# Causal attention with a hard-swish feed-forward on one core: VectorE's bit operations by way of PSUM, the first groups' remainders on GpSimd, batch 0's attention later in the order

## The chip, the cores and the metric

The program runs on one core of a Trainium2 chip. The metric is the device time of one execution, in microseconds. The median of three runs of the kernel before is 700.54 us (698.27 to 700.77). PE is TensorE, DVE VectorE, ACT ScalarE, POOL GpSimd, and SP the engine that issues the DMAs.

## The reference, cut to what matters

```python
def _attn_ref(q, k, v):                    # each (4, 12, 448, 64): batch, head, token, dim
    scores = (1.0 / np.sqrt(64)) * np.matmul(q, k.transpose(0, 1, 3, 2))
    scores = np.where(mask, -1000000000.0, scores)      # causal
    scores = scores - np.max(scores, axis=-1, keepdims=True)
    attn = np.exp(scores)
    attn = attn / (np.sum(attn, axis=-1, keepdims=True) + 1e-09)
    return np.matmul(attn, v)

def _moe_ref(x, w_in, w_out):              # x (1792, 768), w_in (768, 2048), w_out (2048, 768)
    h = x @ w_in
    g = h * np.clip(h + 3.0, 0.0, 6.0) / 6.0
    return g @ w_out
```

## The kernel before

The 1792 tokens go in five groups. Group 0 holds the first 112 tokens of each of the four batches (448 columns); groups 1 to 4 hold the other 336 tokens of one batch each. Heads go in 6 pairs, two of 64 dims on the 128 partitions.

**Attention.** `first_pair` (L294) does one head pair of group 0 for all four batches: scores and mask into two PSUM banks `s` (PE), row maxima on DVE, exponentials on ACT, sums, `inverse` (L365: add 1e-9 and reciprocal, once for each head), the scaling `pr` (L372, POOL or DVE), transposes (L381) through banks `mo`, copies to `pt` (L237 on ACT or L240 on DVE), products with v (L394) into the bank `av`. `pair` (L405) does one pair of a batch's other 336 tokens: six score tiles in banks `s` (L420), a masked maximum on DVE (L437), exponentials on ACT (L444), reciprocals on DVE (L453, L454), scaling on POOL (L466), transposes (L477) through banks `s`, copies to `pt`, products with v (L496) into `av`. There are 24 such pairs, 6 for each batch. `x_split` (L276) then turns `av` into two parts: `xh`, rounded to fp32r (ACT), and the remainder `xl = av - xh` (DVE, L249).

**Feed-forward.** `group` (L553) multiplies 16 chunks of `w_in` (768 columns) by x, and 24 chunks of `w_out` (512 columns) by g. Each product is done in three (`triple`, L547): wh·xh (L549), wh·xl (L550), wl·xh (L551), which makes 576 products for each group. Behind a chunk of `w_in` stand ACT (`r`, ReLU of h + 3), DVE (L579: r = min(r, 6)·h), the rounded `gh` and the remainder `gl = r - gh` (L249).

**Weights.** The inputs are stored as float64 words. In group 0, `weights` (L508) loads a chunk as pairs of int32 (`wd`, 1536 or 1024 columns) and makes float32 of it with three integer operations on DVE (`bits`, L527): L531 shifts and masks the high words into `wf`, L533 ors in the sign bits, L535 ors in the low words' bits. L533 and L535 each read `wd` and `wf`, both in SBUF. Then `wh` is rounded on ACT (L237), `wl = wf - wh` is taken on POOL (L249), and SP writes `wf` to DRAM (`kept`). Groups 1 to 4 load the kept float32 chunks and do no bit operations.

**What sets the order.** `Flow` is a planner that runs when the program is built. Every operation has a key (a due time), the engines that may do it with a cost for each (`{"D": 1, "P": (1.9, .7)}` means DVE, or POOL at 1.9 times the cost and only .7 us after it became ready), and its buffers. The planner gives each engine a fixed list, which the chip follows in order. Group g has keys from 96·g; chunk i of `w_in` has 96·g + 3·i. Pair n of the 24 has key T_REST + 16·n with T_REST = -22, its loads come 24 earlier, and its products with v 13 later. Eight PSUM banks are shared out as `s` 5, `av` 1, `mo` 2.

Of the kernel before, what the change touches and what calls it, by code (L numbers as in the profile page):

```python
# [48 lines left out]

T_FIRST, T_REST, T_LOAD, T_W, T_WLOAD = -66, -22, -24, 9, 9  # L50


BUFS = dict(
    gh=1, gl=1, prow=3, wf=2, r=2, ob=2, qr=3, kr=3, vr=3, wh=3, wl=3, pr3=4, pr2=4, pr1=4,
    pt0=4, pt1=4, pt2=4, wd=4, xh=9, xl=9,
)
BANKS = dict(s=5, av=1, mo=2)

# [131 lines left out]
def tile_causal_attention_hardswish_moe(ctx: ExitStack, tc: tile.TileContext, q, k, v, w_in, w_out, out):  # L190
# [24 lines left out]
    def f(x):  # L215
        return x.bitcast(F32)
# [59 lines left out]
    def x_split(key, g, p, av, n):  # L276
        xh, xl = buf("xh", [128, S], F32R), buf("xl", [128, S], F32R)
        x_t[g, p] = xh, xl
        move(key, n, lambda: ap(xh)[:, :n], lambda: ap(av)[:, :n], [(av, 0)], [(xh, 0)], {"A": 1, "D": (1, .5)})
        minus(  # L280
            key + .01, n, lambda: ap(xl)[:, :n], lambda: ap(av)[:, :n], lambda: f(ap(xh)[:, :n]),
            [(av, 0), (xh, 0)], [(xl, 0)], {"D": 1},
        )
# [8 lines left out]
    def first_pair(p):  # L292
# [112 lines left out]
    def pair(n):  # L405
        b, p = divmod(n, NPAIR)
        t = T_REST + 16 * n
        qr, kr, vr = buf("qr", [128, R]), buf("kr", [128, S]), buf("vr", [C, NC_, 2, D])
# [50 lines left out]
        for e in range(2):  # L459
# [11 lines left out]
            for a, js in enumerate(((0,), (1,), (2, 3))):  # L471
# [3 lines left out]
                def turn(e=e, blocks=blocks, tp=tp):  # L475
# [32 lines left out]
    def weights(g, i, t, early):  # L508
# [3 lines left out]
        if g:  # L512
            dma(t - T_W - T_WLOAD, 512 * n, lambda: f(ap(wd))[:, :n], lambda: kept[i, :, :n], [("kept", i)], [(wd, 0)])
            w, wk = lambda: f(ap(wd))[:, :n], (wd, 0)
        else:
            m, r = divmod(i - NF, 4)
            src = w_in[i] if i < NF else w_out[m, :, 4 * r:4 * r + 4]
            dma(
                early if early else t - T_W - T_WLOAD, 1024 * n,
                lambda: ap(wd)[:, :2 * n].rearrange("p (n k) -> p n k", k=256), lambda: src, [], [(wd, 0)],  # L520
            )
            wf = buf("wf", [128, 768])
            w, wk = lambda: ap(wf)[:, :n], (wf, 0)

            def bits(a):  # L527
                ti = w().bitcast(I32)
                low, high = ap(wd)[:, 0:2 * n:2], ap(wd)[:, 1:2 * n:2]
                if a == 0:  # L530
# [22 lines left out]
    def group(g):  # L553
# [3 lines left out]
        for i in range(NF):  # L557
# [3 lines left out]
            for part in range(3):  # L561
                def products(part=part, wh=wh, wl=wl, acc=acc):
# [13 lines left out]
            )  # L576
            one(
                t, {"D": 1}, elem(n),
                lambda _, r=r, acc=acc: nc.vector.scalar_tensor_tensor(  # L579
                    ap(r)[:, :n], ap(r)[:, :n], 6.0, ap(acc)[:, :n], ALU.min, ALU.mult  # L580
                ),
                [(acc, 0)], [(r, 0)],
            )
# [80 lines left out]
```

## Time and profile before

| | us |
|---|---|
| median of 3 runs | 700.54 |
| the profiled execution, its own time | 699.9 |
| its span, first to last instruction | 698.2 |
| PE busy | 664.2 (95%) |
| DVE busy | 443.3 (63%) |
| ACT busy | 356.3 (51%) |
| POOL busy | 224.7 (32%) |

The shares are means over stages that differ. The first product of group 0 starts 44.6 us after the span's start, the first product of group 0 with `w_out` at 145.9 us, and the first product of group 1 at about 238 us. After that every chunk of weights is a plain load. Matmuls overlap, so that a busy PE is not PE at its peak.

### The profile page before, as it was taken

To read this page: it belongs to the slowest core of one execution; us is meant where nothing else is said; L and a number is where in the kernel's file an instruction comes from. 1 tells how busy PE (TensorE), PEld (TensorE's weight loads), DVE (VectorE), ACT (ScalarE), POOL (GpSimd) and SP (SyncE) were. 2 spreads that over 40 slices of the span, in tenths; PEclk is the share of its full clock that TensorE was granted. 3 is DMA by queue.
4 is the path that set the end of the run, shared out by engine and by line. 5 is a ranking of instruction groups with operands and counts; after the bars stand their busy time and mean duration, and the time that the engine had idled before them with its cause. 6 is when DMAs were issued, how large, how long until landed. Compare 5 with 4: busy or idle time off the path is not lost.

```text
span 698.2 us, 11840 instructions
## 1 busy us (share of the span) xinstructions
PE 664.2 (95%) x4236; PEld 572.1 (82%) x4236; DVE 443.3 (63%) x875; ACT 356.3 (51%) x844; POOL 224.7 (32%) x267
## 2 busy tenths in 40 slices
PE   6788987989999899999999999999999999999998
PEld 4566766768767778889988889988889899999998
DVE  5898998996779466554555666454576643466532
ACT  4665554454235455665555666445576554444332
POOL 2445465553536432322213342201344310022000
PEclk9899999999999999999999999999999999999999
DMA  9958767667787544345564333545533244744452
GB/s 236 289 162 253 227 180 209 194 198 236 220 258 234 162 127 130 88 123 158 164 176 133 115 108 112 173 134 170 158 114 93 77 124 130 209 145 119 138 161 74
DMA packets 60347, 113.63 MB, mean 163 GB/s; under 512 B 14976, under 2 KB 26880, under 8 KB 60288
## 3 DMA queue, kind: packets, MB, share of 16 engines
q1 hardware_dynamic: 60288, 112.88, 54.7%
q8 instruction: 33, 0.54, 0.3%
q14 instruction: 26, 0.21, 0.1%
HBM read 94.77 MB, written 18.09 MB: 162 GB/s over the span
## 4 chain that ended last, share of the span: by engine, by line
PE 66%; POOL 0%; ACT 0%; issue 0%
PE mo L549 18%; PE mo L551 17%; PE mo L550 17%; PE s L420 5%; PE av L496 5%; PE s L477 4%; POOL pr L466 0%; POOL wl L249 0%; ACT ob L237 0%
## 5 line engine op out<-in xcount | busy, mean ns | idle before, releaser
L249 DVE TENSOR_TENSOR wl<-wd,wh 128x512 fp32r<-128x512 f32 (+1 forms) x153 | 124.9, 817 | 151.9 <-ACT wh L237 147.5
L237 ACT CAST wh<-wd 128x512 fp32r<-128x512 f32 (+1 forms) x160 | 112.8, 705 | 151.6 <-PE mo L550 88.7
L549 PE MATMUL mo<-xh,wh 128*128 128x336 f32 (+1 forms) x480 | 164.5, 343 | 3.7 <-DVE r L579 3.7
L549 PE MATMUL mo<-gh,wh 128*128 128x336 f32 (+1 forms) x480 | 164.2, 342 | 0.0
L551 PE MATMUL mo<-gh,wl 128*128 128x336 f32 (+1 forms) x480 | 158.6, 330 | 4.1 <-POOL wl L249 4.0
L550 PE MATMUL mo<-gl,wh 128*128 128x336 f32 (+1 forms) x480 | 157.2, 327 | 0.0
L551 PE MATMUL mo<-xh,wl 128*128 128x336 f32 (+1 forms) x480 | 157.0, 327 | 0.0
L550 PE MATMUL mo<-xl,wh 128*128 128x336 f32 (+1 forms) x480 | 156.6, 326 | 0.0
L466 POOL TENSOR_SCALAR pr<-pr,prow 112x224 f32<-112x224 f32 x144 | 102.4, 730 | 156.3 <-PE mo L550 89.6
L549 PEld LDWEIGHTS mo<-xh,wh 128*128 128x128 f32 x480 | 90.4, 188 | 16.8 <-issue 7.8
L549 PEld LDWEIGHTS mo<-gh,wh 128*128 128x128 f32 x480 | 91.1, 190 | 11.1 <-issue 5.8
L551 PEld LDWEIGHTS mo<-gh,wl 128*128 128x128 f32 x480 | 90.9, 189 | 8.2 <-POOL wl L249 6.6
L550 PEld LDWEIGHTS mo<-gl,wh 128*128 128x128 f32 x480 | 91.2, 190 | 1.3
L551 PEld LDWEIGHTS mo<-xh,wl 128*128 128x128 f32 x480 | 90.4, 188 | 1.8 <-POOL wl L249 0.3
L550 PEld LDWEIGHTS mo<-xl,wh 128*128 128x128 f32 x480 | 90.5, 189 | 1.2
L444 ACT ACTIVATE pr<-s,prow 112x448 f32<-112x448 f32 (+1 forms) x144 | 77.1, 540 | 26.7 <-DVE prow L437 26.7
L249 POOL TENSOR_TENSOR wl<-wf,wh 128x512 fp32r<-128x512 f32 (+1 forms) x39 | 64.5, 1654 | 73.1 <-ACT wh L237 63.1
L437 DVE CUSTOM_DVE_ANT_0 s<-s,mask 112x448 f32<-112x448 f32 (+1 forms) x144 | 69.9, 529 | 10.5 <-PE s L420 10.5
L244 POOL TENSOR_SCALAR gh<-r 128x336 fp32r<-128x336 f32 x52 | 24.5, 471 | 158.8 <-DVE r L579 141.6
L237 ACT CAST wh<-wf 128x512 fp32r<-128x512 f32 (+1 forms) x40 | 28.2, 706 | 76.3 <-DVE wf L535 63.2
L477 PE MATMUL s<-ident,pr 112*112 112x112 f32 x432 | 58.8, 264 | 7.6 <-POOL pr L466 4.8
L237 ACT COPY pt<-s 112x336 f32<-112x336 f32 x133 | 53.5, 440 | 23.1 <-PE s L477 22.0
(57 smaller groups left out, 706.0 us busy)
## 6 DMA issues: line engine op xcount, KB each, us to landing
wd<-kept_w SPq DMA_DIRECT2D x64, 384.0 KB, 3.3
wd<-kept_w SPq DMA_DIRECT2D x96, 256.0 KB, 2.7
wd<-in_w_in_dram SPq DMA_DIRECT2D x16, 768.0 KB, 5.2
wd<-in_w_out_dram SPq DMA_DIRECT2D x24, 512.0 KB, 4.6
kept_w<-wf SPq DMA_DIRECT2D x16, 384.0 KB, 5.5
kept_w<-wf SPq DMA_DIRECT2D x24, 256.0 KB, 4.7
kr<-in_k_dram SPq DMA_DIRECT2D x24, 224.0 KB, 3.4
vr<-in_v_dram SPq DMA_DIRECT2D x24, 224.0 KB, 3.1
```

Of the source, the lines that this page charges most:

```text
L237: nc.scalar.copy(o(), i()) if scale is None else nc.scalar.mul(o(), i(), scale)
L244: nc.gpsimd.tensor_scalar(o(), i(), 1.0, 1.0, ALU.mult, ALU.mult)
L249: (nc.gpsimd if e == "P" else nc.vector).tensor_tensor(o(), a(), b(), ALU.subtract)
L420: nc.tensor.matmul(ap(ps[e, i])[:C, :w], ap(qr)[m, C * (i - 1):C * i], ap(kr)[m, :w], start=True, stop=True)
L437: lambda _, e=e, i=i, w=w, dst=dst: nc.vector.tensor_tensor_reduce(dst(), dst(), mask[:, S - w:], -0.125, 3.0e38, ALU.add, ALU.min, ap(st) ...
L444: lambda _, e=e, i=i, dst=dst: nc.scalar.activation(ap(pr[e, i]), dst(), ACTF.Exp, bias=ap(st)[:, e, i:i + 1], scale=-1.0, accum_out=ap(st ...
L466: nc.gpsimd.tensor_scalar(x, x, r, 1.0, ALU.mult, ALU.mult)
L477: nc.tensor.transpose(ap(tp)[:C, C * o:C * o + C], ap(pr[e, i])[:, C * j:C * j + C], ident)
L496: nc.tensor.matmul(ap(av)[64 * e:64 * e + 64, R - w:R], ap(vr)[:, j, e, :], ap(ph)[:, o:o + w], start=(j == 0), stop=(j == NC_ - 1),)
L549: nc.tensor.matmul(ps, ap(wh)[:, a], xh, start=start, stop=False)
L550: nc.tensor.matmul(ps, ap(wh)[:, a], xl, start=False, stop=False)
L551: nc.tensor.matmul(ps, ap(wl)[:, a], xh, start=False, stop=stop)
```

## The change

It does five things.

1. The first two bit operations of a chunk write their result to a PSUM bank of `s`, and the third reads it there and writes `wf`. A bank holds 512 columns, so that a chunk of `w_in` goes in two halves of 384: six instructions where there were three. A chunk of `w_out` (512) stays at three.
2. In group 0, `gl` goes to POOL first (DVE may take it 1.5 us after it became ready), and `gh` to ACT alone.
3. In groups 0 and 1, `x_split` makes a copy `xf` of the result in SBUF (ACT), and `xl = xf - xh` goes to POOL, or to DVE after 1 us. Groups 2 to 4 stay as they were.
4. Batch 0's pairs have key 4 + 13·n where they had -22 + 16·n (n = 0 to 5: 4 to 69, before -22 to 58), the later pairs -16 + 16·n, and every pair's products with v come 15.9 behind its key, before 13. In batch 0 the copies of `pt` go to ACT alone.
5. `av` has no bank of its own: products with v take one of the banks `s`, of which there are now six. `inverse` of the first pairs does both heads at once.

```diff
-T_FIRST, T_REST, T_LOAD, T_W, T_WLOAD = -66, -22, -24, 9, 9
+T_FIRST, T_EARLY, T_REST, T_LOAD, T_W, T_WLOAD = -66, 4, -16, -24, 9, 9
 BUFS = dict(
-    gh=1, gl=1, prow=3, wf=2, r=2, ob=2, ...
+    gh=1, gl=1, prow=3, wf=2, xf=2, r=2, ob=2, ...
-BANKS = dict(s=5, av=1, mo=2)
+BANKS = dict(s=6, mo=2)
...
         move(key, n, lambda: ap(xh)[:, :n], lambda: ap(av)[:, :n], [(av, 0)], [(xh, 0)], {"A": 1, "D": (1, .5)})
+        y = av
+        if g < 2:
+            y = buf("xf", [128, S])
+            move(key, n, lambda: ap(y)[:, :n], lambda: ap(av)[:, :n], [(av, 0)], [(y, 0)], {"A": 1})
         minus(
-            key + .01, n, lambda: ap(xl)[:, :n], lambda: ap(av)[:, :n], lambda: f(ap(xh)[:, :n]),
-            [(av, 0), (xh, 0)], [(xl, 0)], {"D": 1},
+            key + .01, n, lambda: ap(xl)[:, :n], lambda: ap(y)[:, :n], lambda: f(ap(xh)[:, :n]),
+            [(y, 0), (xh, 0)], [(xl, 0)], {"P": 2, "D": (1, 1.0)} if g < 2 else {"D": 1},
...
+        def inverse(_):
+            r = ap(st)[:, :, 4:8]
+            nc.vector.tensor_scalar_add(r, r, 1e-9)
+            nc.vector.reciprocal(r, r)
+        sums = [(st, 0, 4)] + [(st, 1, 4 + b) for b in range(B)]
+        one(t + 3.5, {"D": 1}, .5, inverse, [], sums)
         for e in (1, 0):
-            def inverse(_, e=e):
-                nc.vector.tensor_scalar_add(row(e, 4), row(e, 4), 1e-9)
-                nc.vector.reciprocal(row(e, 4), row(e, 4))
-            one(t + 3.5, {"D": 1}, .45, inverse, [], sums)
...
-        av = bank("av")
+        av = bank("s")
...
-        t = T_REST + 16 * n
+        t = T_REST + 16 * n if b else T_EARLY + 13 * n
...
-                    [(tp, 0)], [(ph, 0)], {"A": 1, "D": (1, .4)},
+                    [(tp, 0)], [(ph, 0)], {"A": 1, "D": (1, .4)} if b else {"A": 1},
...
-        pe(t + 13, [(1.9, times_v, [(av, 0)])], [(vr, 0)] + [(x[0], 0) for x in pt.values()], True)
-        x_split(t + 13.5, b + 1, p, av, R)
+        pe(t + 15.9, [(1.9, times_v, [(av, 0)])], [(vr, 0)] + [(x[0], 0) for x in pt.values()], True)
+        x_split(t + 16, b + 1, p, av, R)
...
-            for a in range(3):
-                one(t - T_W + .01 * a, {"D": 1}, elem(n) * (.7 if a == 0 else 1.25), lambda _, a=a: bits(a), [(wd, 0)], [wk])
+            def bits(cv, o, m, step):
+                ti = ap(cv)[:, :m].bitcast(I32)
+                low, high = (ap(wd)[:, 2 * o + a:2 * o + 2 * m:2] for a in range(2))
+                if step == 0:
                     nc.vector.tensor_scalar(ti, high, 3, 0x3FFFFFFF, ALU.logical_shift_left, ALU.bitwise_and)
+                elif step == 1:
                     nc.vector.scalar_tensor_tensor(ti, high, -(1 << 30), ti, ALU.bitwise_and, ALU.bitwise_or)
                 else:
-                    nc.vector.scalar_tensor_tensor(ti, low, 29, ti, ALU.logical_shift_right, ALU.bitwise_or)
+                    o = ap(wf)[:, o:o + m].bitcast(I32)
+                    nc.vector.scalar_tensor_tensor(o, low, 29, ti, ALU.logical_shift_right, ALU.bitwise_or)
+            wk = []
+            m = n if n <= 512 else n // 2
+            for o in range(0, n, m):
+                cv = bank("s")
+                wk.append((wf, o))
+                one_by_one = [
+                    (elem(m), lambda _, cv=cv, o=o, a=a: bits(cv, o, m, a), [[(cv, 0)], [(cv, 0)], [(wf, o)]][a])
+                    for a in range(3)
+                ]
+                flow.op(t - T_W + .01, {"D": (1, 0)}, one_by_one, [(wd, 0)])
...
-                {"P": 1.05, "A": (1, .3)} if g else {"A": 1, "P": (1.05, .5)},
+                {"P": 1.05, "A": (1, .3)} if g else {"A": 1},
...
-                [(r, 0), (gh, i)], [(gl, i)], {"D": 1, "P": (1.9, .7)},
+                [(r, 0), (gh, i)], [(gl, i)], {"D": 1, "P": (1.9, .7)} if g else {"P": 2, "D": (1, 1.5)},
```

**How the lists change.** DVE's list before, early in group 0, at the third and fourth chunk of `w_in`:

```order
L531 TENSOR_SCALAR wf<-wd 128x768
L533 SCALAR_TENSOR_TENSOR wf<-wd,wf 128x768
L535 SCALAR_TENSOR_TENSOR wf<-wd,wf 128x768
L531 TENSOR_SCALAR wf<-wd 128x768
L437 ISA s,prow<-s,mask 112x224
L437 ISA prow 112x1
L437 ISA s,prow<-s,mask 112x224
L437 ISA prow 112x1
L533 SCALAR_TENSOR_TENSOR wf<-wd,wf 128x768
L535 SCALAR_TENSOR_TENSOR wf<-wd,wf 128x768
```

Three instructions of 768 columns make one chunk, and a pair's masked maxima (L437, `ISA`) stand between two of a chunk's. Now, at the fourth chunk (numbers tell the buffers apart; L536, L538 and L541 are the new lines of the three steps, L441 is the old L437, L592 the old L579):

```order
L536 TENSOR_SCALAR s_622<-wd_181 128x384
L538 SCALAR_TENSOR_TENSOR s_622<-wd_181,s_622 128x384
L541 SCALAR_TENSOR_TENSOR wf_633<-wd_181,s_622 128x384
L536 TENSOR_SCALAR s_635<-wd_181 128x384
L538 SCALAR_TENSOR_TENSOR s_635<-wd_181,s_635 128x384
L541 SCALAR_TENSOR_TENSOR wf_633<-wd_181,s_635 128x384
L441 ISA s_536,prow_506<-s_536,mask_129 112x224
L441 ISA prow_506 112x1
L592 SCALAR_TENSOR_TENSOR r_655<-r_655,mo_611 128x448
L536 TENSOR_SCALAR s_669<-wd_425 128x384
```

Each half of a chunk has a bank of its own, `s_622` and `s_635`, and its three steps stand one behind the other; only the third writes `wf_633`.

POOL's list before, at the fifth to eighth chunk of `w_in`:

```order
L466 TENSOR_SCALAR pr_720<-pr_720,prow 112x224
L466 TENSOR_SCALAR pr_672<-pr_672,prow 112x336
L466 TENSOR_SCALAR pr_633<-pr_633,prow 112x448
L249 TENSOR_TENSOR wl<-wf,wh 128x768 x4
L249 TENSOR_TENSOR gl<-r,gh 128x448
```

POOL does `wl` of four chunks with nothing between, and one `gl` behind them. Now, at the seventh to ninth chunk (L470 is the old L466):

```order
L470 TENSOR_SCALAR pr_667<-pr_667,prow 112x224
L470 TENSOR_SCALAR pr_618<-pr_618,prow 112x336
L470 TENSOR_SCALAR pr_554<-pr_554,prow 112x448
L249 TENSOR_TENSOR wl<-wf,wh 128x768
L249 TENSOR_TENSOR gl<-r,gh 128x448
L249 TENSOR_TENSOR wl<-wf,wh 128x768
L249 TENSOR_TENSOR gl<-r,gh 128x448
L249 TENSOR_TENSOR wl<-wf,wh 128x768
L249 TENSOR_TENSOR gl<-r,gh 128x448
```

A `gl` stands behind each `wl`. In all of group 0, DVE's list now holds 3 `gl` (before 14), POOL's 13 (before 2). Of the 12 `xl` of groups 0 and 1, POOL has 11 and DVE 1; before, DVE had all 12. DVE's list holds 6 copies `pt` from `mo` (before 2) and 3 scalings L372 (before 1), and its add-and-reciprocal instructions of the first pairs are 12 (before 24).

On PE, the scores of batch 0's first pair and two thirds of those of its second stood ahead of the first product of group 0; now those of the first pair alone. The six products with v of batch 0 stood behind 24, 54, 156, 234, 336 and 432 of group 0's 576 products; now they stand behind 126, 198, 270, 354, 420 and 480.

## Rows read from the trace of the kernel before

**Rows 1.** The page: 40 slices of the span, busy tenths.
```profile
PE   6788987989999899999999999999999999999998
...
DVE  5898998996779466554555666454576643466532
```

**Rows 2.** Stages: us, busy us (count) per engine, clock, DMA share, GB/s.
```profile
0.00:44.60 44.60, 31.93 (x272) 22.32 (x272) 33.44 (x87) 24.52 (x83) 14.66 (x18) 0.92 0.92 242
44.60:145.90 101.30, 89.59 (x474) 69.23 (x472) 95.05 (x141) 54.03 (x125) 56.09 (x43) 0.98 0.68 207
145.90:238.00 92.10, 85.69 (x437) 68.05 (x437) 67.49 (x116) 34.58 (x86) 47.15 (x46) 0.97 0.74 223
238.00:690.00 452.00, 451.99 (x3027) 407.79 (x3026) 246.66 (x533) 242.73 (x549) 106.83 (x160) 1.00 0.46 135
```

**Rows 3.** PE's waits, 44.6 to 145.9 us: total us, times, longest us.
```profile
PE s L477 <- POOL pr L466: 4.3, 8, 1.3
PE mo L549 <- DVE r L579: 3.7, 4, 1.6
PE s L477 <- ACT pt L237: 2.1, 1, 2.1
PE s L420 <- ACT pr L444: 1.6, 1, 1.6
```

**Rows 4.** PE's waits from 145.9 to 238 us.
```profile
PE mo L551 <- POOL wl L249: 4.0, 3, 2.6
PE s L420 <- ACT pr L444: 1.1, 2, 0.7
```

**Rows 5.** DVE groups by form, 0 to 238 us: busy us, mean ns | idle before.
```profile
L533 DVE SCALAR_TENSOR_TENSOR wf<-wd,wf 128x768 int32<-128x768 int32 x16 | 24.8, 1549 | 0.3
L533 DVE SCALAR_TENSOR_TENSOR wf<-wd,wf 128x512 int32<-128x512 int32 x24 | 23.3, 969 | 0.8
L535 DVE SCALAR_TENSOR_TENSOR wf<-wd,wf 128x512 int32<-128x512 int32 x24 | 20.3, 846 | 0.8
L535 DVE SCALAR_TENSOR_TENSOR wf<-wd,wf 128x768 int32<-128x768 int32 x16 | 18.5, 1155 | 0.3
L531 DVE TENSOR_SCALAR wf<-wd 128x512 int32<-128x512 int32 x24 | 17.9, 744 | 16.6 <-DMA kept_w<-wf 5.7 <-POOL wl L249 5.5 <-issue 3.7
L249 DVE TENSOR_TENSOR gl<-r,gh 128x448 fp32r<-128x448 f32 x14 | 16.1, 1153 | 1.5 <-ACT gh L237 1.5
L531 DVE TENSOR_SCALAR wf<-wd 128x768 int32<-128x768 int32 x16 | 13.4, 839 | 3.5 <-DMA kept_w<-wf 3.1 <-POOL pr L466 0.4
...
L240 DVE COPY pt<-mo 112x448 f32<-112x448 f32 x2 | 1.2, 606 | 0.0
```

**Rows 6.** DVE in order of time near 108 us: start us, us, line.
```profile
105.52 0.96 DVE L535 SCALAR_TENSOR_TENSOR wf<-wd,wf 128x768 int32<-128x768 int32 x1
...
107.35 0.55 DVE L531 TENSOR_SCALAR wf<-wd 128x768 int32<-128x768 int32 x1
107.94 2.50 DVE L533 SCALAR_TENSOR_TENSOR wf<-wd,wf 128x768 int32<-128x768 int32 x1
```

**Rows 7.** POOL in order of time, the same microseconds.
```profile
107.75 1.87 POOL L249 TENSOR_TENSOR wl<-wf,wh 128x768 fp32r<-128x768 f32 x1 [4.03 <-ACT wh L237]
```

**Rows 8.** One SBUF operand: ns min/median/max of `r` (group 0) and `xl` (run).
```profile
L579 DVE SCALAR_TENSOR_TENSOR r<-r,mo x16: 603/610/618, 57.5 to 152.3; 128x448 f32<-128x448 f32 x16
L249 DVE TENSOR_TENSOR xl<-av,xh x30: 467/507/624, 18.9 to 584.9; 128x336 fp32r<-128x336 f32 x24, 128x448 fp32r<-128x448 f32 x6
```

**Rows 9.** POOL groups by form, 0 to 238 us.
```profile
L249 POOL TENSOR_TENSOR wl<-wf,wh 128x768 fp32r<-128x768 f32 x15 | 32.3, 2155 | 35.3 <-ACT wh L237 27.8 <-DMA kr<-in_k_dram 3.8 <-PE mo L551 1.8
...
L249 POOL TENSOR_TENSOR gl<-r,gh 128x448 fp32r<-128x448 f32 x2 | 2.8, 1400 | 0.0
```

**Rows 10.** PE in order of time, before the first product of group 0.
```profile
28.07 1.04 PE L324 MATMUL s<-gh 64*112 64x112 f32 x16 [2.07 <-DMA gh<-in_k_dram]
...
41.09 2.66 PE L420 MATMUL s<-kr,qr 64*112 64x448 f32 x8
```

More of the change, by code (lines that the diff above doesn't have):

```diff
@@ L47 @@
 NCHUNK = NF + 4 * NK
-T_FIRST, T_REST, T_LOAD, T_W, T_WLOAD = -66, -22, -24, 9, 9
+T_FIRST, T_EARLY, T_REST, T_LOAD, T_W, T_WLOAD = -66, 4, -16, -24, 9, 9
 BUFS = dict(
-    gh=1, gl=1, prow=3, wf=2, r=2, ob=2, qr=3, kr=3, vr=3, wh=3, wl=3, pr3=4, pr2=4, pr1=4,
+    gh=1, gl=1, prow=3, wf=2, xf=2, r=2, ob=2, qr=3, kr=3, vr=3, wh=3, wl=3, pr3=4, pr2=4, pr1=4,
     pt0=4, pt1=4, pt2=4, wd=4, xh=9, xl=9,
 )
-BANKS = dict(s=5, av=1, mo=2)
+BANKS = dict(s=6, mo=2)
 class Buf:
@@ L360, in first_pair @@
         )
-        for e in (1, 0):
-            sums = [(st, 1, 4 + b) for b in range(B)] if e else [(st, 0, 4)]
-            def inverse(_, e=e):
-                nc.vector.tensor_scalar_add(row(e, 4), row(e, 4), 1e-9)
-                nc.vector.reciprocal(row(e, 4), row(e, 4))
-            one(t + 3.5, {"D": 1}, .45, inverse, [], sums)
+        def inverse(_):
[4 more added lines that the diff above has]
+        one(t + 3.5, {"D": 1}, .5, inverse, [], sums)
+        for e in (1, 0):
             one(
@@ L489, in pair @@
                     o += w
-        av = bank("av")
+        av = bank("s")
         def times_v():
@@ L513, in weights @@
             dma(t - T_W - T_WLOAD, 512 * n, lambda: f(ap(wd))[:, :n], lambda: kept[i, :, :n], [("kept", i)], [(wd, 0)])
-            w, wk = lambda: f(ap(wd))[:, :n], (wd, 0)
+            w, wk = lambda: f(ap(wd))[:, :n], [(wd, 0)]
         else:
@@ L522, in weights @@
             wf = buf("wf", [128, 768])
[L523 to L530, printed above, removed]
+            w = lambda: ap(wf)[:, :n]
+            def bits(cv, o, m, step):
+                ti = ap(cv)[:, :m].bitcast(I32)
+                low, high = (ap(wd)[:, 2 * o + a:2 * o + 2 * m:2] for a in range(2))
+                if step == 0:
                     nc.vector.tensor_scalar(ti, high, 3, 0x3FFFFFFF, ALU.logical_shift_left, ALU.bitwise_and)
-                elif a == 1:
+                elif step == 1:
                     nc.vector.scalar_tensor_tensor(ti, high, -(1 << 30), ti, ALU.bitwise_and, ALU.bitwise_or)
                 else:
-                    nc.vector.scalar_tensor_tensor(ti, low, 29, ti, ALU.logical_shift_right, ALU.bitwise_or)
-            for a in range(3):
-                one(t - T_W + .01 * a, {"D": 1}, elem(n) * (.7 if a == 0 else 1.25), lambda _, a=a: bits(a), [(wd, 0)], [wk])
-            dma(t - T_W, 512 * n, lambda: kept[i, :, :n], w, [wk], [("kept", i)])
-        move(t - T_W + .1, n, lambda: ap(wh)[:, :n], w, [wk], [(wh, 0)], {"A": 1})
+                    o = ap(wf)[:, o:o + m].bitcast(I32)
[10 more added lines that the diff above has]
+                flow.op(t - T_W + .01, {"D": (1, 0)}, one_by_one, [(wd, 0)])
+            dma(t - T_W, 512 * n, lambda: kept[i, :, :n], w, wk, [("kept", i)])
+        move(t - T_W + .1, n, lambda: ap(wh)[:, :n], w, wk, [(wh, 0)], {"A": 1})
         minus(
-            t - T_W + .2, n, lambda: ap(wl)[:, :n], w, lambda: f(ap(wh))[:, :n], [wk, (wh, 0)], [(wl, 0)],
+            t - T_W + .2, n, lambda: ap(wl)[:, :n], w, lambda: f(ap(wh))[:, :n], wk + [(wh, 0)], [(wl, 0)],
             {"D": 1.15, "P": (2, .5)} if g else {"P": 2, "D": (1.15, 2.0)},
@@ L576, in group, with gate @@
             )
[L577 to L583, printed above, removed]
+            def gate(_, r=r, acc=acc):
+                nc.vector.scalar_tensor_tensor(ap(r)[:, :n], ap(r)[:, :n], 6.0, ap(acc)[:, :n], ALU.min, ALU.mult)
+            one(t, {"D": 1}, elem(n), gate, [(acc, 0)], [(r, 0)])
             move(
                 t, n, lambda i=i: ap(gh)[:, i, :n], lambda r=r: ap(r)[:, :n], [(r, 0)], [(gh, i)],
-                {"P": 1.05, "A": (1, .3)} if g else {"A": 1, "P": (1.05, .5)},
+                {"P": 1.05, "A": (1, .3)} if g else {"A": 1},
             )
```

## The prediction

> **What bounds the kernel now.** I read the page's slices first [rows 1]. PE is at nine tenths from the second third on, with gaps only in the first third, and in that third DVE is the fullest engine. So I cut the span at the events named in the table above and read each stage [rows 2]. From 238 to 690 us PE is busy 451.99 of 452.00 us while DVE is busy 246.66 (55%): nothing that another engine does faster can shorten this stage. Before it, PE is idle 44.60 - 31.93 = 12.7 us, then 101.30 - 89.59 = 11.7 us (while `w_in` is multiplied), then 92.10 - 85.69 = 6.4 us (`w_out`). The granted clock is 0.92, 0.98 and 0.97 of full speed there, and 1.00 later. This is all that the change can reach: 18.1 us of idle time and, by the clock, 101.3 x 0.02 + 92.1 x 0.03 = 4.8 us in the second and third stage, and part of the first.
>
> Who is late? In the second stage PE waits for POOL's scaling (4.3), for DVE's `r` (3.7), for a copy (2.1) and for a pair's exponentials (1.6) [rows 3]; in the third for POOL's `wl` (4.0) and for exponentials (1.1) [rows 4]. Three of these hang on DVE, which is busy 95.05 of 101.30 us in the second stage: `r` is its own, POOL's scaling needs DVE's reciprocals, and `wl` needs the bit operations.
>
> DVE is so full because its instructions are stretched. An undisturbed bit operation of 768 columns takes 0.96 us, and L531 0.55 us. The same L533 takes 2.50 us when it starts at 107.94 [rows 6]; POOL's `wl` started at 107.75 and ran 1.87 us [rows 7], and the 2.50 us are the 1.7 that were left of it plus some 0.8 to 0.9 of work. So a DVE instruction with two operands in SBUF stands still while POOL works. The groups show it in the mean: L533 1549 ns, L535 1155, L531 839, `gl` 1153 [rows 5]. An instruction with one operand in PSUM and one in SBUF never does: 16 `r` lie between 603 and 618 ns, and 30 `xl` of two sizes between 467 and 624 [rows 8].
>
> **The change part by part.**
>
> *Bit operations.* All 40 chunks cost DVE 24.8 + 23.3 + 20.3 + 18.5 + 17.9 + 13.4 = 118.2 us now [rows 5]. Undisturbed, a chunk of 768 columns would take 0.55 + 0.96 + 0.96 = 2.5 us, one of 512 two thirds of it or 1.7: 16 x 2.5 + 24 x 1.7 = 81 us, so 37 us are standstill. The trace has no integer operation on PSUM. The nearest rows are `r` and `xl`: 610 ns for 448 columns, 507 for 336, or 0.92 ns a column [rows 8], which gives 551 ns for 384 columns and 669 for 512. Against the first step's price stands that a copy from PSUM takes 606 ns for 448 columns [rows 5], so I take the same for all three steps; the low end for the first is half of 0.55 us. New cost: 16 x 6 x 0.551 + 24 x 3 x 0.669 = 52.9 + 48.2 = 101.1 us, or 17.1 us less. This holds only if the standstill goes, since without it the new form is 20 us dearer than the old.
>
> The Trainium skill, "VectorE: DVE Perf Modes", section on why PSUM operands drop a tier, says that an operand in PSUM takes float32 instructions to one element a cycle, where a single-source one between SBUF buffers does two. The trace agrees: 0.55 us for 768 columns against 0.606 for 448. By that rule alone the change makes DVE slower, and the time would be that of the third rival.
>
> *Moves off DVE.* 11 `gl` at 1.153 us: 12.7 us less. 11 `xl`, 6 at 0.61 and 5 at 0.51: 6.2 less. 4 copies more at 0.606: 2.4 more. Two scalings more, priced like a `gl` with its two SBUF operands: 2.3 more. The 12 small instructions less I leave at nothing. With the bit operations DVE loses 17.1 + 12.7 + 6.2 - 2.4 - 2.3 = 31.3 us of the 33.44 + 95.05 + 67.49 = 196.0 us before 238. Half or more of that falls into the second stage, so DVE has at most 80 us of work there.
>
> *On to POOL.* 11 `gl` of 448 columns at 1.40 us as the two now [rows 9], or at 1.87 x 448 / 768 = 1.09 undisturbed: 12 to 15 us. 11 `xl` at 0.8 to 1.4 us: 9 to 15. POOL is busy 14.66 + 56.09 + 47.15 = 117.9 us of 238; it gets 21 to 30 more, less 15 x (2.155 - 1.87) = 4.3 us of its own standstill [rows 7, 9]. That leaves it at about 60% over the three stages and 75% in the second. ACT has 24.5, 54.0 and 34.6 us of work in the stages [rows 2]; the 12 copies `xf` add some 6 us, which its idle time covers. If that cover were gone, a copy of 0.5 us would sit between a pair's products and its `xl`.
>
> *PE's waits.* I take the waits one by one. `r` stands behind stretched instructions: 3.2 of 3.7 us go. POOL's scaling waits for reciprocals on a shorter queue: 3.0 of 4.3. `wl`: its bit operations come sooner, but POOL has a `gl` behind every `wl`: 2.0 of 4.0. Exponentials: 1.4 of 2.7, as fewer pairs meet the first chunks and `s` has a bank more. The copy: 2.0 of 2.1, since batch 0's copies leave DVE. Together 11.6 of the 18.1 us; the bounds are 0 and 18.1.
>
> *The clock.* Of the 4.8 us I take 2.0, because part of the low clock lies in idle time, where it costs nothing. Bounds 0 and 4.8.
>
> *The start.* The last keys arrive at 28.07 us, after PE has waited 2.07 us for them, with the DMA engines at 0.92 of the stage [rows 2, 10]; the loads ahead of them are the same. Between that and 44.6 us lies a chain through DVE that loses the `xl`, most of the masked maxima of one and a half pairs, and gains copies and scalings. The second pair's scores, 2.66 us on PE at 41.09 [rows 10], leave for later, where they still must be done. Net I take 1.5 us, with bounds of -1 and 4.
>
> *Later stages.* Batch 0's last products with v have 96 of group 0's products behind them before group 1 needs them, some 30 us at the third stage's pace (92.1 us for half of the 576) [rows 2]; I cost the later keys at nothing. What covers that is this distance; if it were gone, PE would wait at 238 us for one pair's chain.
>
> **Sum.** 11.6 + 2.0 + 1.5 = 15.1 us off the profiled execution's own 699.9 us: 684.8. That execution lies 0.6 us under the median, less than this sum can resolve, so the forecast is **685 us**. Its own range runs from 674 (all idle time of the two stages, the clock, and 3 us at the start: 25.9 us) to 693.
>
> **The rivals.**
>
> 1. *POOL takes DVE's place.* POOL gets up to 30 us, and each `wl` has a `gl` beside it and each scaling may have both ahead of it: 1.4 + 1.87 us of queue, more than the longest wait for a scaling today, 1.3 us [rows 3]. For it: half of PE's waits are for POOL already. Against it: POOL is under 80% in the fullest stage, and DVE may take a `gl`. Price: the idle time stays and only the start's 1.5 us are won: 698 us.
>
> 2. *The banks run out (slower).* The ring `s` now feeds a pair's six score tiles, its six transposes, its products with v and, in group 0, 56 bit conversions. The rows that bear on it are PE's waits for exponentials, which free a score bank: 1.6 us at the longest [rows 3]. If each of the 18 pairs after batch 0 lost that, the stage where PE now never waits would grow by 28.8 us: 685 + 29 = 714 us. It decides from 15.1 / 18 = 0.84 us a pair. Against it: there is one bank more in the ring, the bit conversions end with group 0, and with `s` at five PE has no wait in 452 us.
>
> 3. *The change doesn't do what it says.* The standstill could belong to the reads of `wd` rather than to the second SBUF operand. Then the 37 us stay and the new form costs 20 more: DVE has 138 us of bit operations, 20 more than now, and gives 18.9 away with `gl` and `xl`. Its load is what it was: 700 us. Against it: `r` and `xl` are never stretched, and `gl`, which doesn't read `wd`, is.
>
> **How the numbers follow.** The forecast has 0.70; all of its own range is over 0.5% faster (below 697), and 0.5% is about what a measurement of this kernel can tell from no change. Rival 1 has 0.17: 0.04 of it falls below 697, the rest is the same. Rival 2 has 0.08, slower. Rival 3 has 0.05, nearly all of it the same and 0.01 slower. So faster 0.74, same 0.17, slower 0.09. The range runs from 674 to 699, so that it takes in the first rival and leaves out the other two.
>
> **What would show it.** In the profile after, L538 and L541 at 0.55 us (384 columns) and 0.67 us (512) without a long tail, however busy POOL is; `wl` of 768 columns near 1.87 us; DVE under nine tenths in the slices from 45 to 130 us; PE's idle time between the first product of group 0 and the first of group 1 at some 6 us, before 18; group 1 starting near 224 us; no waits from there to the end. I am wrong if L538 is stretched as L533 was, if PE's waits for POOL rise above 8 us before group 1, or if PE waits for banks after it.

## The result, and the profile after

The changed kernel takes 675.07 us (median of 4 runs, 672.09 to 675.96), the kernel before 699.40 in the same comparison (4 runs, 695.77 to 700.77): a ratio of 0.9652 with an interval of 0.9602 to 0.9702. That is faster by 24 us, at the low end of the range given, and 10 us more than forecast. The profiled execution is one of 672.09 us with a span of 670.4, which is 27.8 less than the span before (698.2). It is the fastest of the four, so that these 27.8 us are 3.5 more than the medians differ; the accounts below are made against these two spans.

The page of the kernel after, 40 slices of the span, busy tenths, as in [rows 1]:

```profile
PE   7489999999999999999999999999999999999998
DVE  5998899776766667454475663445757543566432
```

The gaps of PE after the third slice are gone. DVE is under nine tenths from the eighth slice on (117 us), where before it stood at eight or nine tenths from the second slice to the ninth (157 us). One event of [rows 2] has to be put right first. 238 us is not where group 1 starts in the kernel before: its first product with 336 columns stands at 223.61, twelve of them run among group 0's last ones, and 238 us is the end of group 0's products.

```profile
223.61 0.31 PE L549 MATMUL mo<-xh,wh 128*128 128x336 f32 x1
```

In the changed kernel the first product of group 1 starts at 202.70 us, and group 0's products end at 211.15. The stages are cut at the first product of group 0, the first of `w_out` (0.16 us ahead of it) and the first of group 1; the fourth row has the third stage to the end of group 0's products, which is the cut of [rows 2]. Columns as there:

```profile
0.00:45.77 45.77, 30.69 (x264) 21.87 (x264) 36.76 (x77) 23.82 (x79) 18.75 (x22) 0.93 0.94 261
45.77:124.60 78.83, 77.64 (x428) 64.02 (x427) 70.84 (x158) 48.38 (x113) 55.49 (x50) 1.00 0.75 231
124.60:202.70 78.10, 78.10 (x446) 63.41 (x445) 55.94 (x113) 38.32 (x95) 44.51 (x49) 1.00 0.85 257
124.60:211.15 86.55, 86.55 (x493) 70.89 (x491) 60.51 (x127) 43.76 (x109) 47.14 (x51) 1.00 0.84 255
202.70:662.00 459.30, 458.70 (x3071) 415.00 (x3071) 254.78 (x550) 248.97 (x567) 106.70 (x163) 1.00 0.46 137
```

The second stage took 101.30 us and takes 78.83; the third, to the end of group 0's products, took 92.10 and takes 86.55. Most of the gain lies in the second. PE's idle time in the two went from 18.1 us to 1.2, and the granted clock from 0.98 and 0.97 to 1.00. The first stage is 1.2 us longer, with 15.1 us of idle time where there were 12.7.

PE's waits over the whole run (total us, times, longest us), against [rows 3, 4]:

```profile
PE mo L385 <- DVE pr L376: 6.5, 2, 5.5
PE s L328 <- DMA gh<-in_k_dram: 3.2, 3, 1.6
PE s L321 <- DVE maskr L272: 2.3, 1, 2.3
PE mo L563 <- DVE r L592: 1.8, 4, 0.8
```

Only the last of these lies behind 45.77 us. Nothing is left of the waits for POOL's scaling and `wl`, and nothing took their place; a new one of 5.5 us, for a scaling of the first pairs (L376), stands in the first stage.

DVE's groups by form, 0 to 202.7 us (busy us, mean ns | idle before), against [rows 5]; L536, L538 and L541 are the three steps:

```profile
L538 DVE SCALAR_TENSOR_TENSOR s<-wd,s 128x384 int32<-128x384 int32 x32 | 18.0, 562 | 1.1
L536 DVE TENSOR_SCALAR s<-wd 128x384 int32<-128x384 int32 x32 | 17.8, 557 | 0.9 <-ACT pr L347 0.6
L541 DVE SCALAR_TENSOR_TENSOR wf<-wd,s 128x384 int32<-128x384 int32 x32 | 17.7, 554 | 3.7 <-DMA kept_w<-wf 2.1
L536 DVE TENSOR_SCALAR s<-wd 128x512 int32<-128x512 int32 x24 | 16.9, 705 | 0.0
L538 DVE SCALAR_TENSOR_TENSOR s<-wd,s 128x512 int32<-128x512 int32 x24 | 16.7, 697 | 0.8
L541 DVE SCALAR_TENSOR_TENSOR wf<-wd,s 128x512 int32<-128x512 int32 x24 | 16.5, 688 | 13.2 <-DMA kept_w<-wf 9.6 <-POOL pr L470 2.2
```

They cost 103.6 us together, before 118.2. And the tail is gone (ns min/median/max of L538, both sizes):

```profile
L538 DVE SCALAR_TENSOR_TENSOR s<-wd,s x56: 561/564/716, 17.8 to 201.5; 128x384 int32<-128x384 int32 x32, 128x512 int32<-128x512 int32 x24
```

On POOL in the same stretch, `wl` of 768 columns takes 1.86 us in the mean where it took 2.155 [rows 9], and `gl` 1.16 where the two of before took 1.40:

```profile
L249 POOL TENSOR_TENSOR wl<-wf,wh 128x768 fp32r<-128x768 f32 x16 | 29.7, 1858 | 22.8 <-issue 11.5 <-ACT wh L237 9.2 <-POOL gl L249 0.9
...
L249 POOL TENSOR_TENSOR gl<-r,gh 128x448 fp32r<-128x448 f32 x13 | 15.0, 1158 | 0.3 <-ACT gh L237 0.2
```

**Where the 27.8 us came from.** PE executes the same 4236 instructions in both traces. Its idle time fell from 34.0 us to 20.1 (16.9 won in the two stages, 2.4 lost at the start, 0.5 at the end). The clock took 7.6 us of PE's busy time before and 2.3 now (one less the granted clock, times PE's busy time, summed over stretches of 2 us). Together that is 19.3 us. The other 8.5 lie in time that the profile counts as busy, at a granted clock of 1.00; they come up again below.

### The profile page after: what moved, and what is told of

Its sections match the earlier page's. It is cut to its first block, busy times and chain, and to the rows that moved or that the text cites. A ratio compares the mean times of both kernels' runs of the same rounds, so it can differ in the third digit from the quotient of the medians.

```text
span 670.4 us, 11916 instructions
## 1 busy us (share of the span) xinstructions
PE 650.3 (97%) x4236; PEld 569.2 (85%) x4236; DVE 419.0 (63%) x896; ACT 360.1 (54%) x855; POOL 225.5 (34%) x283
## 4 chain that ended last, share of the span: by engine, by line
PE 90%; DVE 6%; DMA 2%; issue 1%; ACT 0%; SPq 0%; DVEq 0%
PE mo L563 25%; PE mo L565 23%; PE mo L564 23%; PE s L424 7%; PE s L500 7%; PE s L481 6%; DMA kept_w<-wf 1%; DVE s L538 1%; DVE prow L335 1%; DMA gh<-in_k_dram 1%; DVE s L536 1%; DVE wf L541 1%; DVE prow L341 1%; DVE pt L240 0%; DVE s L441 0%
## 5 line engine op out<-in xcount | busy, mean ns | idle before, releaser
L249 DVE TENSOR_TENSOR wl<-wd,wh 128x512 fp32r<-128x512 f32 (+1 forms) x157 | 128.9, 821 | 143.9 <-ACT wh L237 143.5
L563 PE MATMUL mo<-gh,wh 128*128 128x336 f32 (+1 forms) x480 | 162.0, 338 | 0.0
L565 PE MATMUL mo<-gh,wl 128*128 128x336 f32 (+1 forms) x480 | 156.6, 326 | 0.0
L470 POOL TENSOR_SCALAR pr<-pr,prow 112x224 f32<-112x224 f32 x144 | 93.5, 668 | 154.0 <-PE mo L564 132.6
L441 DVE CUSTOM_DVE_ANT_0 s<-s,mask 112x448 f32<-112x448 f32 (+1 forms) x144 | 70.4, 530 | 26.2 <-PE s L424 26.2
L244 POOL TENSOR_SCALAR gh<-r 128x336 fp32r<-128x336 f32 x53 | 26.2, 495 | 162.3 <-DVE r L592 158.3
L249 POOL TENSOR_TENSOR wl<-wf,wh 128x512 fp32r<-128x512 f32 (+1 forms) x40 | 61.2, 1531 | 51.7 <-ACT wh L237 36.8
L237 ACT COPY pt<-s 112x336 f32<-112x336 f32 x131 | 52.1, 443 | 34.8 <-PE s L481 34.6
L481 PE MATMUL s<-ident,pr 112*112 112x112 f32 x432 | 55.2, 259 | 0.0
L424 PE MATMUL s<-kr,qr 64*112 64x224 f32 (+2 forms) x288 | 54.3, 481 | 0.2 <-ACT xf L237 0.2
```

What stands on the lines that cost most here:

```text
L237: nc.scalar.copy(o(), i()) if scale is None else nc.scalar.mul(o(), i(), scale)
L244: nc.gpsimd.tensor_scalar(o(), i(), 1.0, 1.0, ALU.mult, ALU.mult)
L249: (nc.gpsimd if e == "P" else nc.vector).tensor_tensor(o(), a(), b(), ALU.subtract)
L424: nc.tensor.matmul(ap(ps[e, i])[:C, :w], ap(qr)[m, C * (i - 1):C * i], ap(kr)[m, :w], start=True, stop=True)
L441: lambda _, e=e, i=i, w=w, dst=dst: nc.vector.tensor_tensor_reduce(dst(), dst(), mask[:, S - w:], -0.125, 3.0e38, ALU.add, ALU.min, ap(st) ...
L470: nc.gpsimd.tensor_scalar(x, x, r, 1.0, ALU.mult, ALU.mult)
```

## The experiments

Four questions: is the gain the end of the standstill, or that of the moves, the order, or the banks? And why did the start not get shorter?

**The undo: everything as changed, but the intermediate back in SBUF.** The lists of PE and POOL are those of the changed kernel, line for line; only the place of the first two steps' result differs.

```diff
+    pools["cs"] = ctx.enter_context(tc.tile_pool(name="cs", bufs=4))
...
-                ti = ap(cv)[:, :m].bitcast(I32)
+                ti = inter(cv)[:, :m].bitcast(I32)
```

> The changed kernel with the same lists on PE and POOL and the same instructions on DVE; only the intermediate of the bit operations lies in SBUF instead of a PSUM bank. Theory A (the gain is the end of DVE's standstill beside POOL): the second and third step have two SBUF operands again, their means for 384 columns go from 0.56 us to 0.8 or more with single ones over 1.5 us, PE's waits before group 1 return, and the time rises from 675 by 10 us or more, to 685 to 700. Rival B (the gain is work taken off DVE by the moves of gl and xl): the steps cost the same or less (0.4 to 0.55 us), the time stays under 679. Rival C (the gain is the later place of batch 0's attention): likewise under 679.

Measured: 697.90 us (696.31 to 699.38, 10 runs), ratio to the kernel before 0.9996 (0.9975 to 1.0017). All of the gain is gone. Its DVE groups by form, 0 to 230 us (L544 is L538 of the changed kernel, L547 L541, L542 L536), and L544's spread:

```profile
L544 DVE SCALAR_TENSOR_TENSOR cs<-wd,cs 128x384 int32<-128x384 int32 x32 | 32.8, 1026 | 1.1
...
L547 DVE SCALAR_TENSOR_TENSOR wf<-wd,cs 128x384 int32<-128x384 int32 x32 | 25.5, 797 | 1.8
...
L542 DVE TENSOR_SCALAR cs<-wd 128x384 int32<-128x384 int32 x32 | 21.3, 665 | 0.0
```

```profile
L544 DVE SCALAR_TENSOR_TENSOR cs<-wd,cs x56: 558/824/3301, 17.3 to 227.7; 128x384 int32<-128x384 int32 x32, 128x512 int32<-128x512 int32 x24
```

The fastest L544 takes 558 ns, what the PSUM form takes; but the mean of the 384-column ones is 1026. In order of time, on DVE and then on POOL (start us, us):

```profile
109.58 0.56 DVE L547 SCALAR_TENSOR_TENSOR wf<-wd,cs 128x384 int32<-128x384 int32 x1
110.06 0.36 DVE L542 TENSOR_SCALAR cs<-wd 128x384 int32<-128x384 int32 x1
110.45 2.12 DVE L544 SCALAR_TENSOR_TENSOR cs<-wd,cs 128x384 int32<-128x384 int32 x1
```

```profile
110.30 1.86 POOL L255 TENSOR_TENSOR wl<-wf,wh 128x768 fp32r<-128x768 f32 x1 [4.53 <-ACT wh L243]
```

Alone, the steps take 0.36 and 0.56 us; beside POOL's `wl`, which ends at 112.16, the second ends at 112.57. The same picture as [rows 6, 7], in the new program. What the standstill does to PE is in its waits and stages:

```profile
PE mo L569 <- DVE r L598: 11.2, 8, 2.5
...
PE mo L569 <- ACT wh L243: 3.7, 2, 3.5
```

```profile
46.10:144.50 98.40, 84.22 (x428) 69.15 (x427) 93.68 (x156) 48.10 (x112) 62.18 (x49) 0.93 0.61 185
144.50:226.20 81.70, 79.75 (x445) 62.75 (x445) 74.43 (x113) 39.03 (x96) 52.84 (x49) 1.00 0.79 245
```

DVE is full again, `r` is late, and the clock falls to 0.93. Against the changed kernel, with the same PE list and both traces cut at the first product of group 1, the second stage is 19.6 us longer and the third 3.6, of 24.9 us in all (span 695.3). By the account used above 16.1 us of this are idle time and 9.4 the clock. So the theory of the standstill holds: the moves to POOL, the later keys and the shared banks, all still in, win nothing without the PSUM.

**The reverse: the kernel before with the bit operations through PSUM.** With them come the six banks `s` that feed products with v too; `gl`, `xl`, the keys and the copies are as before.

```diff
-        t = T_REST + 16 * n if b else T_EARLY + 13 * n
+        t = T_REST + 16 * n
...
-        pe(t + 15.9, [(1.9, times_v, [(av, 0)])], [(vr, 0)] + [(x[0], 0) for x in pt.values()], True)
+        pe(t + 13, [(1.9, times_v, [(av, 0)])], [(vr, 0)] + [(x[0], 0) for x in pt.values()], True)
```

(against the changed kernel; `T_REST`, `x_split`, `gl`, `gh`, `pt` and `inverse` likewise back to the lines before.)

> The kernel before with one part of the change: bit operations by way of PSUM, and for that the six shared banks; gl, xl and the order's keys as before. Theory A: most of the gain comes, 682 to 690 us (before 699.4), L538's kind at 0.56 and 0.70 us without a tail. Rival B: DVE keeps its gl and xl and its bit operations are nominally dearer, so 697 or more. Rival C: 697 or more.

Measured: 677.27 us (674.80 to 680.71, 4 runs), ratio 0.9691 (0.9642 to 0.9740). This alone gives 21 us, nearly all of the gain and more than was expected. PE's waits, in a profiled execution that is the slowest of the four (680.71 us):

```profile
PE s L477 <- DVE wf L537: 5.7, 3, 2.8
...
PE s L420 <- DVE wf L537: 1.4, 1, 1.4
```

Here is what the second rival feared: transposes and scores wait until a bit conversion gives its bank back (L537 is its last step), 7.1 us in all. It is bounded, because it ends with group 0's conversions. In the changed kernel PE never waits for a bit conversion's bank; its one wait for a bank is 0.2 us (scores, for the copy `xf`).

**All but the moves.** `gl`, `xl`, `gh` and the copies `pt` where they were, the rest as changed.

```diff
-        if g < 2:
+        if g < 0:
...
-            [(y, 0), (xh, 0)], [(xl, 0)], {"P": 2, "D": (1, 1.0)} if g < 2 else {"D": 1},
+            [(y, 0), (xh, 0)], [(xl, 0)], {"D": 1},
...
-                [(r, 0), (gh, i)], [(gl, i)], {"D": 1, "P": (1.9, .7)} if g else {"P": 2, "D": (1, 1.5)},
+                [(r, 0), (gh, i)], [(gl, i)], {"D": 1, "P": (1.9, .7)},
```

> The changed kernel without its moves: gl and xl on DVE first as before, no xf, gh and the copies with the old choices; PSUM intermediates, banks and keys as changed. Theory A: gl's standstill is back, the rest is kept: 678 to 686 us. Rival B: 690 or more. Rival C: 678 or less.

Measured: 676.93 us (676.37 to 678.13, 4 runs), ratio 0.9700 (0.9663 to 0.9737). That is under the 678 to 686 expected, and by the number alone it falls where theory C was put; what rules C out is the undo, and the run with the old keys below. The interval overlaps that of the changed kernel; the moves are worth about 2 us or nothing.

**All but the later keys.** All pairs' keys (batch 0's, and -22 for -16 in the later ones) and the distance of the products with v as before.

```diff
-T_FIRST, T_EARLY, T_REST, T_LOAD, T_W, T_WLOAD = -66, 4, -16, -24, 9, 9
+T_FIRST, T_REST, T_LOAD, T_W, T_WLOAD = -66, -22, -24, 9, 9
...
-        t = T_REST + 16 * n if b else T_EARLY + 13 * n
+        t = T_REST + 16 * n
...
-        pe(t + 15.9, [(1.9, times_v, [(av, 0)])], [(vr, 0)] + [(x[0], 0) for x in pt.values()], True)
-        x_split(t + 16, b + 1, p, av, R)
+        pe(t + 13, [(1.9, times_v, [(av, 0)])], [(vr, 0)] + [(x[0], 0) for x in pt.values()], True)
+        x_split(t + 13.5, b + 1, p, av, R)
```

> The changed kernel with the old keys: pairs at -22 + 16 n, products with v 13 behind. Theory A: 676 to 684 us, some DVE work of two pairs comes back before the first product of group 0, which then starts 2 to 4 us later. Rival C: 690 or more. Rival B: as theory A.

Measured: 674.41 us (673.27 to 675.17, 4 runs), ratio 0.9660 (0.9623 to 0.9697). That is faster than the 676 to 684 expected: the later keys are worth nothing that can be measured. Group 0's first product then starts at 51.45 us, 5.7 later than in the changed kernel, and the time is the same: what stands ahead of the first product has to be done sometime. Banks: PE waits 1.6 us for L541 here (0.9 in transposes, 0.7 in scores) and 0.6 us in the run without the moves, against 7.1 in the reverse, which has neither. So the moves or the keys, either one, take most of these waits away, and both together win no more.

**The start, first: the small scaling on ACT.** In the first stage of the changed kernel a four-column instruction takes 2.35 us on DVE (start us, us; DVE, then POOL):

```profile
27.76 1.11 DVE L368 TENSOR_SCALAR prow<-prow 112x8 f32<-112x8 f32 x1
28.90 0.20 DVE L369 RECIPROCAL prow<-prow 112x8 f32<-112x8 f32 x1
29.02 0.58 DVE L335 TENSOR_REDUCE prow<-s 112x4 f32<-112x448 f32 x1
29.64 2.35 DVE L341 TENSOR_SCALAR prow<-prow 112x4 f32<-112x4 f32 x1
```

```profile
27.71 1.13 POOL L249 TENSOR_TENSOR xl<-xf,xh 128x448 fp32r<-128x448 f32 x1 [1.40 <-ACT xf L237]
29.27 0.93 POOL L376 TENSOR_TENSOR pr<-pr,prow 112x448 f32<-112x448 f32 x1 [0.43 <-DVE prow L369]
30.17 1.80 POOL L249 TENSOR_TENSOR wl<-wf,wh 128x768 fp32r<-128x768 f32 x1
```

L368 ends at 28.87 with POOL's `xl` (28.84), L341 at 31.99 with POOL's `wl` (31.97). In the kernel before, the same scaling of four columns (there L337) took 0.14 us, with no `xl` on POOL:

```profile
29.98 0.14 DVE L337 TENSOR_SCALAR prow<-prow 112x4 f32<-112x4 f32 x1
```

(The six of that line before lie between 0.14 and 0.58 us, so that some were held then too.) The reduction between them runs beside POOL's L376 and is not held; the reciprocal falls into POOL's idle time and tells nothing. The edit takes L341 off DVE:

```diff
-                    t + 1, {"D": 1}, .25,
-                    lambda _: nc.vector.tensor_scalar(row(1, 0), row(1, 0), -0.125, None, ALU.mult),
+                    t + 1, {"A": 1}, .25,
+                    lambda _: nc.scalar.mul(row(1, 0), row(1, 0), -0.125),
```

> The changed kernel with the four-column scaling of the row maxima (L341) done by ACT instead of DVE. In the changed kernel one such instruction stood 2.35 us beside POOL's work, and PE then waited 5.5 us for DVE's scaling L376, the longest wait left. Theory S (what is left in the start is the same standstill, now of small two-port instructions beside the xl that POOL was given): the 5.5 us wait falls under 3.5 us, the first product of group 0 starts 1.5 to 3 us sooner than 45.8, time 671 to 674. Rival T (the start is bound by the loads and by DVE's amount of work): first product within 1 us of 45.8 and 674 to 677.

Measured: 674.16 us (673.69 to 676.31, 5 runs), ratio 0.9662 (0.9635 to 0.9689). PE's wait for L376 shrinks, but the waits for loads grow, and group 0 starts at 47.08 us. That the small scaling sets the start is not borne out:

```profile
PE s L328 <- DMA gh<-in_k_dram: 4.9, 5, 2.1
PE mo L385 <- DVE pr L376: 4.0, 1, 4.0
```

**The start, second: group 0's `xl` back on DVE**, so that POOL holds nothing up there.

```diff
-        if g < 2:
+        if g == 1:
...
-            [(y, 0), (xh, 0)], [(xl, 0)], {"P": 2, "D": (1, 1.0)} if g < 2 else {"D": 1},
+            [(y, 0), (xh, 0)], [(xl, 0)], {"P": 2, "D": (1, 1.0)} if g == 1 else {"D": 1},
```

> The changed kernel with the xl of group 0 back on DVE, from PSUM, without their xf copies. Theory S: POOL is free of 1.15 us instructions in the start, L341 no longer stands still, and the 6 x 0.61 us that DVE gets are about paid back: 672 to 677. Rival T: DVE's amount of work sets the start, which grows by 3 us or more: 678 or more.

Measured: 673.26 us (671.84 to 675.04, 4 runs), ratio 0.9639 (0.9611 to 0.9666). L376's wait falls to 2.8 us and the first product starts at 46.00, as late as ever. Giving these six `xl` to POOL won nothing.

**A bank of its own for the products with v.**

```diff
-BANKS = dict(s=6, mo=2)
+BANKS = dict(s=5, av=1, mo=2)
...
-        av = bank("s")
+        av = bank("av")
```

(the last in both places.)

> The changed kernel with a bank of its own for products with v and five in the ring s, as before the change. If sharing the banks mattered (the sixth bank is what lets conversions and pairs live beside each other): 679 or more with waits of PE for banks before group 1. If not: 673 to 677.

Measured: 676.55 us (675.57 to 677.10, 4 runs), ratio 0.9683 (0.9658 to 0.9708). PE waits 0.2 us for a conversion's bank here. If the sharing is worth something it is a microsecond or two; the intervals overlap.

**The start, third: L341 and the copies of the first pairs on ACT.** The edit of the first of these three, and:

```diff
-                {"A": 1, "D": (1, .3)},
+                {"A": 1},
```

> As the run with the scaling of the maxima on ACT, and the first pairs' copies pt from mo on ACT alone (DVE had six of them at 0.6 us). Theory S and theory T both let the start shrink if DVE is what it waits for: first product at 42 to 44.5 us and 670 to 673.5. If ACT is the chain there (the copies then queue behind exponentials), 674 or more.

Measured: 672.43 us (670.66 to 674.58, 5 runs), ratio 0.9632 (0.9605 to 0.9659): the lowest median of all, but its interval lies within that of the changed kernel, so that it can't be called faster. The first product starts at 47.65 us. PE's waits are spread over others:

```profile
PE s L328 <- DMA gh<-in_k_dram: 4.7, 4, 1.8
PE s L398 <- ACT pr L448: 2.4, 1, 2.4
...
PE s L424 <- DMA kr<-in_k_dram: 2.1, 1, 2.1
PE mo L385 <- DVE pr L376: 1.4, 1, 1.4
```

The long wait is gone (5.5 to 1.4 us) and the start is no shorter: take one link away and the next is as late. What bounds the first 46 us stays open; no run here moved the loads.

## Why the prediction was right, and where it was off

**The mechanism was right.** An operand in PSUM ends the standstill, the first rival (POOL takes DVE's place) and the third (the standstill belongs to the reads of `wd`) are out, and the second (the banks run out) did not come: PE waits 0.2 us for a bank in the changed kernel. The undo shows that without the PSUM nothing of the gain is left, the reverse that the PSUM nearly suffices. The Trainium skill, "SBUF — State Buffer", section on who interferes with whom, says that VectorE and GpSimd share a pair of SBUF ports under an exclusive lock, and that VectorE needs it when it has two inputs in SBUF, or for a `tensor_scalar` in a two-port mode. The traces agree on both: L544 at 2.12 us for 0.56 beside `wl`, and L341 at 2.35 us for 0.14. The other rule, that of the Trainium skill, "VectorE: DVE Perf Modes", section on why PSUM operands drop a tier, was right of one instruction (L536 of 384 columns takes 557 ns, L542 between SBUF buffers 0.36 us undisturbed). It made a wrong forecast of the time, since beside POOL the mean of L542 is 665.

**The prices were right.** 384 columns at 0.551 us forecast, 0.554 to 0.562 measured; 512 at 0.669, measured 0.688 to 0.705; together 101.1 forecast, 103.6 measured. DVE has 168.1 us of work up to the end of group 0's products, where the terms gave 196.0 - 31.3 = 164.7; it was to have at most 80 in the second stage and has 70.84. One sign was read too simply: DVE's share was to fall under nine tenths from 45 to 130 us, and in the sixth and seventh slices it stays there. The load fell, but the stage it is divided by fell with it (70.84 of 78.83 us is 90%, before 94%); PE, at 77.64, now sets the pace. POOL was to be busy about 60% of the three stages and 75% of the second: 121.4 of 211.15 us (57%), and 55.49 of 78.83 (70%). That the shares came near is in part luck: the terms gave POOL 135 to 144 us of work, and it has 121.4. The stretch of `wl` went, as forecast, but so did one that was left out: the scalings of 224 columns took 737 ns in the mean (L466, 16 of them) and take 458 (L470, 14 of them).

**The step that failed is the sum: what PE gains from a DVE that is on time.** Three terms.

- *PE's waits*, 11.6 us of 18.1: 16.9 went. I kept back 6.5 us wait by wait: half of `wl`'s, half of the exponentials'. But these were not waits with causes of their own. They go with one thing, DVE's load in a stage that PE's own work fills for some 78 us. Over the ten traces PE's idle time in this stage is 11.7 and 14.2 us where DVE has 95.1 and 93.7 us of work (before, undo), 4.2 and 2.0 where it has 80.0 and 78.1 (reverse, no moves), and 0 to 1.2 where it has 66 to 73, but for 2.7 with a bank of its own for `av`.
- *The clock*, 2.0 us of 4.8: all of it went, the two stages stand at 1.00. The reason for keeping half back was that the low clock lay in idle time. It lay in the busy time behind it: there it took 4.9 us, in idle time 0.2. The kernel before, in order of time (start us, us), and in stretches of one microsecond with the columns of [rows 2]:

```profile
44.91 0.36 PE L550 MATMUL mo<-xl,wh 128*128 128x448 f32 x1
45.11 0.37 PE L551 MATMUL mo<-xh,wl 128*128 128x448 f32 x1
...
119.69 0.31 PE L477 MATMUL s<-ident,pr 112*112 112x112 f32 x1 [1.28 <-POOL pr L466]
120.60 0.88 PE L477 MATMUL s<-ident,pr 112*112 112x112 f32 x7 [0.60 <-POOL pr L466]
...
122.27 0.57 PE L549 MATMUL mo<-xh,wh 128*128 128x448 f32 x1
122.64 0.57 PE L550 MATMUL mo<-xl,wh 128*128 128x448 f32 x1
```

```profile
122.00:123.00 1.00, 1.00 (x4) 0.89 (x3) 0.97 (x2) 0.07 (x1) 1.00 (x2) 0.50 0.93 377
123.00:124.00 1.00, 1.00 (x6) 0.82 (x5) 1.00 (x1) 0.00 (x0) 1.00 (x1) 0.50 0.29 117
```

  Behind two waits of 1.28 and 0.60 us PE runs at a granted clock of 0.50, which is 1.2 GHz, with a product every 0.37 us; from 44.91 to 45.72 us, with the same 448 columns, they started every 0.20. PE is busy 1.00 of 1.00 us, so the wait is paid twice, and the second time it doesn't show as idle.
- *The start*, 1.5 us won: 1.2 lost. The 12 small instructions less, left "at nothing", were nothing in the sum: the scalings and reciprocals of the first pairs cost DVE 7.3 us in 18 instructions (L341, L368, L369), before 7.7 in 30. What the sum passed over is that a single one can be long: L368 and L341 stand still beside POOL's new `xl` and its `wl`, and the wait of 5.5 us for L376 is behind them. But the three runs on the start cut that wait to between 1.4 and 4.0 us without a shorter start, so that this explains where PE waited, and not why the start is no shorter. Which part of this term failed stays open.

With these three sizes the sum would have been 16.9 + 4.8 - 1.2 = 20.5 us, or 679. The measured 675 lies at the very end of the range, because more was won in a place that no term names: PE's busy time at full clock.

**The term that was missing** is some 8 us that PE is busy for in the kernel before and not in the changed one, at a granted clock of 1.00. Half of it can be read from the rows. In an unbroken row a product starts every 0.20 us and is shown busy for 0.36 (the rows at 44.91 and 45.11), so that the last one before a break shows some 0.16 us more than its turn takes. In the second and third stage PE breaks off 28 times before (some breaks are of hundredths of a microsecond) and twice now. Set against the usual distance between starts for each form of instruction, that is 4.8 us before and 0.3 now. A wait is thus paid at its beginning too, in time that counts as busy. By the same reckoning another 4 us in the two stages are starts that come late with no idle time shown (6.9 us before, 2.8 now). What held them stays open: in the undo, where DVE is late again, they are 2.9. Such an account is good to a few microseconds at most. PE's busy time less the clock's part is 656.5 us before and 648.0 in the changed kernel, but over the other eight traces, all with the same 4236 instructions, it runs from 642.7 (last run) to 651.2 (old keys).

The moves were priced into DVE's load with 18.9 us (12.7 of `gl`, 6.2 of `xl`), more than the bit operations' 17.1. The load came out near the forecast, but by the third experiment the moves are worth about 2 us in time or nothing. Once DVE was ahead of PE, more spare time on it bought nothing. The later keys, costed at nothing, are worth nothing.

## What to carry to other kernels

When a VectorE instruction's mean is far above its minimum and GpSimd works at the same time, look for a second SBUF operand (or a two-port `tensor_scalar`, however small) and send one side through PSUM; here dearer instructions (20 us more by the undisturbed prices) made the kernel 21 us faster by themselves. Price a wait of TensorE at more than its idle time: the instruction before a break fills its whole length, and the granted clock behind it may fall. Don't price waits that hang on one full engine one by one: they go together. And once the engine that was late is ahead, stop: the other parts of this change, each sensible, were worth 2 us more or nothing.

## What the runs showed that I had not expected

- A scaling of four columns, 0.14 us alone, stood 2.35 us beside GpSimd. It stood through the rest of one GpSimd instruction (L376, to 30.20 us) and the whole of the next (`wl`, to 31.97): a standstill is as long as GpSimd's work, not as VectorE's own. Single ones were held before the change too (L366, four columns, up to 1.16 us).
- GpSimd had lost as well: `wl` of 768 columns went from 2.155 us to 1.86, and the scalings of 224 columns from 0.74 to 0.46. The undo, with the same list on GpSimd, shows what held them: with the intermediate back in SBUF they take 1.92 and 0.62 us, and `gl` 1.32 where the changed kernel has 1.16.
- With more work on GpSimd and the intermediate in SBUF, the bit operations of the undo cost 152.5 us of VectorE (its six groups, 0 to 230 us), where they cost 118.2 before. The halves of 384 columns explain 16 x (2 x (0.36 + 0.56 + 0.56) - (0.55 + 0.96 + 0.96)) = 7.8 us of that by undisturbed prices; the rest is taken to be more standstill, beside more work on GpSimd.
- VectorE still waits 9.6 us for the write-back of `wf` (the row of L541, 512 columns, above). PE is idle for 1.2 us in the two stages, so that it can have lost little by it.
